# A new order of the front's parts, rests of k and v as two tokens per partition, and squares of eight units summed by VectorE, in a planned attention and mixture kernel

## The chip, the cores and the metric

The kernel runs on one core of a Trainium2 chip. The metric is the time of one execution on the device in microseconds (us), the median of several runs. A profile of one further execution comes with it; its instructions, transfers and waits are what the views below show. Engines are named as in the profile: PE is TensorE (PEld its weight loads), DVE is VectorE, ACT is ScalarE, POOL is GpSimd, SP is SyncE, whose queue issues nearly all transfers (SPq).

## What is computed

Linear attention without a softmax, each row normed, then two feed-forward blocks. The reference, cut to its core (batch 4, 8 heads, 576 tokens, head size 64; 2304 tokens of 512 values, 1024 hidden values, 4 experts; all float32, but the four weights of the first block are float64 on the host):

```python
kv = np.einsum('bhsd,bhse->bhde', k, v)
out = np.einsum('bhsd,bhde->bhse', q, kv)
rms = np.sqrt(np.mean(out * out, axis=-1, keepdims=True) + 1e-06)
x = (out / rms * g_norm)            # then to tokens x (heads, head size)
h = (x @ w1) * (x @ w2) @ w3
x = h @ w_out
p = domain_probs / (domain_probs.sum(-1, keepdims=True) + 1e-09)
for e in range(4):
    y += p[:, e:e + 1] * (np.maximum(x @ e_w1[e], 0.0) @ e_w2[e])
```

## The kernel before

**The planner.** The kernel's work is a list of operations. `Plan.add` (line 110) notes for each the engines that may do it, with a cost in us for each of them, what it reads and writes, and a latency after which its result counts as there. `Plan.order` (line 141) plays these costs through and writes out a fixed order for every engine: an engine that is free takes, of the operations that are ready in that play, the one with the lowest stage, not more than `WINDOW` = 14 stages ahead of the first open one, if the buffers it needs are within their limits (99 tiles of 128x512, 9 of them for attention inputs, 12 for decoded weights, 5 raw weights, 8 PSUM banks). An operation with two possible engines goes to the one that would be done first. On the chip each engine then runs its order from the first to the last, waiting on semaphores where an operand is not there.

**The stages.** `FRONT` (line 37) lists the parts of the first third of the kernel; the place in the list is the stage. A part that needs another one that stands later (a weight, a tile of w_out) makes it then and there, and the later entry does nothing. The parts are:

- `unit b p` (line 691): two heads of batch b. It loads q, k and v of 512 tokens, four per partition (256 KB each), and adds up the outer products k'v on TensorE (`outer`, line 706, the matmuls of line 715). The 64 tokens that 512 leaves over (the rest, `REM`) come from a tile that all units of a batch share. Then q is set by tokens, turned on TensorE, multiplied with k'v (`inner`, line 743) and normed.
- `rest_kv b` (line 565), called by the first unit of a batch: two tiles (k and v), in each of which 64 partitions hold a token and 512 columns hold all eight heads; the other 64 partitions are set to zero by GpSimd. Each load is 512 pieces of 256 bytes.
- `normed_turned` (line 577): squares and their sums per head, `root` on GpSimd (lines 606 and 607), the scaling on VectorE (line 610), turning, and splitting into a high and a low part. While fewer than `SUMMING` = 18 units have been made, and there are 18 with the two of the rests, ScalarE does squares and sums: eight passes over 64 columns, each with an accumulated sum (line 594). In the other branch ScalarE squares 512 columns in one pass and VectorE sums them.
- `rest_unit g` (line 753): the 64 last tokens of two batches.
- `weight n f` (line 909): a 512 KB load of float64 columns of w1 or w2, decoded by ScalarE and VectorE.
- `bilinear_plain`, `bilinear_pair`: the products of x with w1 and w2 (line 325 to 327, three matmuls each for high and low parts), the pair ones by a Strassen-Winograd scheme for two batches; `row`: a row of w3 times w_out; `mixed`, `mixed_product`: the second half of the first block.

Behind the front stand the experts' products, in the order of a loop at the end of the kernel; the planner orders them with the same figures. At the start ten warm-up matmuls are issued (line 422), and PSUM banks that units of stages 1 to 3 take get two or three extra matmuls each (`FILL`, line 1728).

Of the kernel before, what the change touches and what calls it, by code (L numbers as in the profile page):

```python
# [18 lines left out]
P = 128  # L19
# [7 lines left out]
SEVEN = (1,)  # L27
DEFERRED = (0,)
PLAIN = 1
SUMMING = 18  # L30
WARM = 10
FILL = {1: 3, 2: 3, 3: 2}
START = 0.7
# [1 line left out]
BIAS = {"dve": 1.0, "act": 0.0, "pool": 1.0, "pe": 0.0, "sp": 0.0}  # L35

FRONT = (
# [12 lines left out]
)  # L50

class Buf:
# [45 lines left out]
class Plan:  # L98
# [8 lines left out]
        self.limits = dict(limits)  # L107
        self.stage = 0

    def add(self, engines, emit, reads=(), writes=(), latency=0.2, stage=None, free=False, hold=None):  # L110

        op = Op(engines, emit, self.stage if stage is None else stage, latency)
        op.hold = hold
        op.ported = {e for e in engines if e == "pool" or (e == "dve" and not free)}
        op.pinned = stage is not None
        for accesses, write in ((reads, False), (writes, True)):  # L120
            for access in accesses:
                buf, key = access if isinstance(access, tuple) else (access, None)
                if buf not in op.bufs:
                    op.bufs.append(buf)
                    buf.users += 1
                for other, k, w in buf.touched:
                    if other is not op and (write or w) and (k is None or key is None or k == key):
                        op.deps.append(other)
                buf.touched.append((op, key, write))
        op.index = len(self.ops)  # L130
        self.ops.append(op)
        return op
# [128 lines left out]
def attention_moe_kernel(  # L261
# [26 lines left out]
    nc = tc.nc  # L288
    B, H, S, D = q.shape
# [3 lines left out]
    HP = H // 2  # L293
    KD = DM // P
    KF = FF // P
    R = 4
    M = R * P
    REM = S - M
# [12 lines left out]
    add = plan.add  # L311
# [7 lines left out]
    def half(name, dt=F32, ring=None):  # L319
        return Buf("h", name, [P, 512], dt, ring)  # L320
# [8 lines left out]
    def t_act(n, psum=False):  # L329
        return (0.157 if psum else 0.19) + n / 1200  # L330

    def t_dve(n):
        return 0.143 + n / 960
# [10 lines left out]
    def load(buf, *parts, key=None, queue="sp", cost=None):  # L344
        def emit(_):
            for dst, src in parts:
                (nc.sync if queue == "sp" else nc.scalar).dma_start(
                    out=dst(buf.tile), in_=src[:, :] if isinstance(src, Buf) else src
                )

        add(
            {queue: cost or (1.48 if buf.kind == "r" else 0.68)}, emit,
            reads=[src for _, src in parts if isinstance(src, Buf)], writes=[(buf, key)], latency=2.6,
        )

    def spilled(name, buf, value=whole, later=0):
# [192 lines left out]
    kvr = {}  # L549
# [6 lines left out]
    def head_pair(src, b, p):  # L556
        return src[b, 2 * p:2 * p + 2, 0:M, :].rearrange("h (p r) d -> p h r d", r=R)
# [4 lines left out]
    def rest(src, b):  # L562
        return src[b, :, M:S, :].rearrange("h p d -> p h d")

    def rest_kv(b):

        kvr[b] = [half("kvr") for _ in (k, v)]
        for raw, src in zip(kvr[b], (k, v)):
            add({"pool": 0.4}, lambda _, raw=raw: nc.gpsimd.memset(raw[REM:P], 0.0), writes=[(raw, 1)])
            load(  # L570
                raw, (lambda t: t[0:REM].rearrange("p (h d) -> p h d", d=D), rest(src, b)),
                key=0, cost=1.05,
            )

    summed = []

    def normed_turned(ps, places, whole_values=None):
# [4 lines left out]
        t = half("x")  # L582
        ss = Buf("n", "ss", [P, 8, 1], F32)

        summing = SUMMING > len(summed)
        summed.append(t)

        def square(e):
# [25 lines left out]
            )  # L614

        if summing:
            add({"act": 8 * t_act(D, True)}, square, reads=[ps], writes=[t, ss])
        else:
            add({"act": t_act(512, True)}, square, reads=[ps], writes=[t])
            add({"dve": t_dve(512)}, total, reads=[t], writes=[ss], free=True)  # L620
        add({"pool": 1.91}, root, writes=[ss], hold=0.3)
        add({"dve": t_dve(512)}, scale, reads=[ps, ss], writes=[t], free=True)
        pt = turned(t)
        if whole_values is not None:

            def scaled(e):
# [9 lines left out]
                reads=[pt, xscale], writes=[whole_values], free=True,  # L636
# [4 lines left out]
        for n, dst, to, value, key in places:  # L641
# [9 lines left out]
            def low(e, dst=dst, to=to, value=value):  # L651
# [7 lines left out]
                reads=[pt, xscale], writes=[(dst.high, key)], free=True,  # L659
# [5 lines left out]

    def zeroed(name):
        t = half(name)
        add({"pool": 0.5}, lambda _: nc.gpsimd.memset(t.tile, 0.0), writes=[t])
        return t

    def evacuate(dst, src, n, to, value, key=None):
# [19 lines left out]
    def unit(b, p):  # L691
        first = b not in kvb
        if first:
            kvb[b] = zeroed("kvb")
        loaded = []
        for name, src in (("q", q), ("kv", k), ("kv", v)):
            raw = half(name, ring="attention")
            load(raw, (heads, head_pair(src, b, p)), cost=0.82)
            loaded.append(raw)
        qraw, ks, vs = loaded  # L700
        if first:
            rest_kv(b)
        kr, vr = kvr[b]
        ps = bank()

        def outer(e):
            for r in range(R + 1):
                for h in range(2):
                    c = slice(h * D, (h + 1) * D)
                    if r < R:  # L710
                        a, b_ = heads(ks.tile)[:, h, r, :], heads(vs.tile)[:, h, r, :]
                    else:
                        m = slice(p * P + h * D, p * P + (h + 1) * D)
                        a, b_ = kr[:, m], vr[:, m]
                    nc.tensor.matmul(ps[c, c], a, b_, start=r == 0, stop=r == R)  # L715

        add({"pe": 0.9}, outer, reads=[ks, vs, kr, vr], writes=[ps])
        for i in range(2):
            c = slice(i * D, (i + 1) * D)
            evacuate(  # L720
                kvb[b], ps, D, lambda t, i=i, c=c: t[c, p * P + i * D:p * P + (i + 1) * D],
                lambda t, c=c: t[c, c], key=(p, i),
            )
        qs = half("qs")

        def by_token(t):
            return t.rearrange("p (r h d) -> p h r d", r=R, h=2)

        add(
            {"act": t_act(512), "dve": t_fast(512)},  # L730
            lambda e: nc.scalar.copy(by_token(qs.tile), heads(qraw.tile)) if e == "act"
            else nc.vector.tensor_copy(out=by_token(qs.tile), in_=heads(qraw.tile)),
            reads=[qraw], writes=[qs],
        )
        pq = turned(qs)
        qt = half("qt")
        evacuate(qt, pq, 512, whole, whole)
        po = bank()

        def inner(e):  # L740
            for r in range(R):
                c = slice(r * P, (r + 1) * P)
                nc.tensor.matmul(po[:, c], qt[:, c], kvb[b][:, p * P:(p + 1) * P], start=True, stop=True)  # L743

        add({"pe": 0.86}, inner, reads=[qt, (kvb[b], (p, 0)), (kvb[b], (p, 1))], writes=[po])
        xr[b, p] = half("xr")
        if b == B - 1 and p < HP // 2:
            normed_turned(po, [], xr[b, p])
        else:
            xt[b, p] = Pair("xt")  # L750
            normed_turned(po, [(512, xt[b, p], whole, whole, None)], xr[b, p])

    def rest_unit(g):
# [1 line left out]
        load(  # L755
            qraw,
            (lambda t: t[0:REM].rearrange("p (h d) -> p h d", d=D), rest(q, 2 * g)),
            (lambda t: t[REM:P].rearrange("p (h d) -> p h d", d=D), rest(q, 2 * g + 1)), cost=1.5,
        )
        pq = turned(qraw)  # L760
        qs = []
# [999 lines left out]
```

## Time and profile before

| | |
|---|---|
| median of three runs | 1110.79 us (1110.38 to 1113.55) |
| the profiled execution | 1111.78 us |
| its span, first to last instruction | 1110.0 us |
| TensorE busy | 1099.5 us (99%), 6964 matmuls |
| VectorE, ScalarE, GpSimd busy | 824.3, 613.2, 47.1 us |
| mean granted clock of TensorE | 0.997 |
| moved | 282.37 MB in 176866 packets |

The span is what the profile covers; the execution's own time is 1.8 us longer. Busy shares are averages over a kernel with different stages, and a TensorE that counts as busy may be running matmuls that only fill time, or running at a lower clock. So the stages have to be looked at one by one, and the waits beside the busy times.

### The profile page before, as it was taken

The numbers are of one execution on the slowest core, as the hardware profiler recorded it, in microseconds if no ns is written. First come the engines' busy times: TensorE is split into PE (matmuls) and PEld (weight loads), VectorE is DVE, ScalarE is ACT, GpSimd is POOL, SyncE is SP. The second block draws the span as 40 slices with busy tenths as digits, with TensorE's granted clock in tenths as the row PEclk, the third lists the DMA queues.
The fourth block names the chain that finished last, engine by engine and source line by source line (L and its number), as shares of the span: only waits on it lengthen the run. The fifth ranks groups of instructions, "written<-read, shape, count | busy, mean of one in ns | idle before, by whom it ended". The sixth has DMA issues, their size and how long they took to land.

```text
span 1110.0 us, 19707 instructions
## 1 busy us (share of the span) xinstructions
PE 1099.5 (99%) x6964; PEld 1025.2 (92%) x6964; DVE 824.3 (74%) x1698; ACT 613.2 (55%) x1501; POOL 47.1 (4%) x57
## 2 busy tenths in 40 slices
PE   8999999999999999999999999999999999999998
PEld 7888888888888998999999999999999999999998
DVE  5888897889869887888888884456488655464783
ACT  6998744556636655754564465444364545443540
POOL 4513200000000000000000000000000000000000
PEclk9999999999999999999999999999999999999999
DMA  9999993450230499999999997778779787696746
GB/s 288 290 341 331 377 349 110 137 164 25 96 95 29 159 324 354 353 314 299 346 355 361 356 363 242 253 230 275 242 259 350 250 262 263 206 318 200 265 141 201
DMA packets 176866, 282.37 MB, mean 254 GB/s; under 512 B 22144, under 2 KB 89728, under 8 KB 176768
## 3 DMA queue, kind: packets, MB, share of 16 engines
q1 hardware_dynamic: 176448, 280.85, 76.0%
q8 instruction: 55, 0.90, 0.3%
q10 hardware_dynamic: 320, 0.26, 0.1%
q14 instruction: 43, 0.35, 0.1%
HBM read 198.22 MB, written 82.84 MB: 253 GB/s over the span
## 4 chain that ended last, share of the span: by engine, by line
PE 93%; DMA 3%; ACT 2%; DVE 1%; issue 0%; POOL 0%; SPq 0%; ACTq 0%; DVEq 0%
PE b L325 30%; PE b L327 30%; PE b L326 30%; PE b L686 2%; PE b L743 1%; DMA weh<-w 1%; DMA w3raw<-in_moe_w_dram 1%; PE b L715 1%; ACT x L594 0%; DMA w<-w2kept 0%; DMA graw<-in_g_norm_dram 0%; DMA we<-wel 0%; DMA e2raw<-in_moe_w_dram 0%; DMA woraw<-in_moe_w_out_dram 0%; PE b L778 0%
## 5 line engine op out<-in xcount | busy, mean ns | idle before, releaser
L327 PE MATMUL b<-w,htl 128*128 128x256 f32 x756 | 213.6, 283 | 0.0
L325 PE MATMUL b<-w,hth 128*128 128x256 f32 x756 | 213.4, 282 | 0.2 <-DMA w<-w2kept 0.2
L326 PE MATMUL b<-w,hth 128*128 128x256 f32 x756 | 213.5, 282 | 0.0
L674 ACT COPY u<-b 128x384 f32<-128x384 f32 (+1 forms) x191 | 96.2, 504 | 200.8 <-PE b L327 199.4
L1408 DVE TENSOR_TENSOR u<-u,b 128x384 f32<-128x384 f32 x144 | 79.6, 553 | 143.7 <-ACT u L674 74.0
L325 PEld LDWEIGHTS b<-w,hth 128*128 128x128 f32 x756 | 144.1, 191 | 0.6 <-DMA w<-w2kept 0.5
L327 PEld LDWEIGHTS b<-w,htl 128*128 128x128 f32 x756 | 144.5, 191 | 0.0
L326 PEld LDWEIGHTS b<-w,hth 128*128 128x128 f32 x756 | 144.2, 191 | 0.0
L1598 DVE SCALAR_TENSOR_TENSOR acc<-b,pn,acc 128x256 f32<-128x256 f32 x165 | 69.7, 478 | 45.2 <-PE b L327 45.2
L1419 ACT ACTIVATE u<-u 128x384 f32<-128x384 f32 x108 | 56.9, 527 | 65.0 <-DVE u L1408 64.8
L370 ACT CAST hth<-s 128x384 fp32r<-128x384 f32 x144 | 70.6, 511 | 28.4 <-DVE s L1508 26.5
L375 DVE TENSOR_TENSOR htl<-s,hth 128x384 fp32r<-128x384 f32 x144 | 75.4, 550 | 1.6 <-ACT hth L370 1.2
L375 DVE TENSOR_TENSOR htl<-u,hth 128x384 fp32r<-128x384 f32 x108 | 56.1, 551 | 13.5 <-ACT hth L370 13.5
L327 PE MATMUL b<-wdh,htl 128*128 128x512 f32 x144 | 56.7, 394 | 0.0
L326 PE MATMUL b<-wdl,hth 128*128 128x512 f32 x144 | 56.6, 393 | 0.0
L325 PE MATMUL b<-wdh,hth 128*128 128x512 f32 x144 | 56.0, 389 | 0.0
L370 ACT CAST hth<-u 128x384 fp32r<-128x384 f32 x108 | 52.8, 512 | 3.2 <-PE b L327 2.6
L325 PE MATMUL b<-th,weh 128*128 128x512 f32 x112 | 44.6, 398 | 1.1 <-ACT u L674 1.1
L327 PE MATMUL b<-th,wel 128*128 128x512 f32 x112 | 43.7, 390 | 0.0
L326 PE MATMUL b<-tl,weh 128*128 128x512 f32 x112 | 43.7, 390 | 0.0
L954 DVE TENSOR_TENSOR u<-u,b 128x512 f32<-128x512 f32 x42 | 28.6, 686 | 17.1 <-PE b L327 9.2
L1508 DVE TENSOR_TENSOR s<-u 128x384 f32<-128x384 f32 x72 | 38.2, 551 | 0.3 <-ACT u L1419 0.2
(290 smaller groups left out, 3000.2 us busy)
## 6 DMA issues: line engine op xcount, KB each, us to landing
w<-w2kept SPq DMA_DIRECT2D x126, 512.0 KB, 4.4
we<-we SPq DMA_DIRECT2D x240, 256.0 KB, 5.4
we<-weh SPq DMA_DIRECT2D x48, 256.0 KB, 4.1
we<-wel SPq DMA_DIRECT2D x48, 256.0 KB, 4.0
e2raw<-in_moe_w_dram SPq DMA_DIRECT2D x40, 256.0 KB, 4.6
w3raw<-in_moe_w_dram SPq DMA_DIRECT2D x16, 512.0 KB, 3.7
e1raw<-in_moe_w_dram SPq DMA_DIRECT2D x32, 256.0 KB, 4.6
w2kept<-wth SPq DMA_DIRECT2D x32, 256.0 KB, 4.4
```

Source lines behind the costliest of these rows:

```text
L325: nc.tensor.matmul(ps, w[0], x[0], start=first, stop=False, skip_group_check=more)
L326: nc.tensor.matmul(ps, w[0], x[1], start=False, stop=False, skip_group_check=more)
L327: nc.tensor.matmul(ps, w[1], x[0], start=False, stop=last, skip_group_check=more)
L370: nc.scalar.copy(to(dst.high.tile), value(src.tile))
L375: nc.vector.tensor_tensor(out=to(dst.low.tile), in0=value(src.tile), in1=to(dst.high.tile), op=ALU.subtract)
L674: lambda e: nc.scalar.copy(to(dst.tile), value(src.tile)) if e == "act"
L686: nc.tensor.transpose(ps[:, c], raw[:, c], ident)
L954: lambda _: nc.vector.tensor_tensor(out=t.tile, in0=t.tile, in1=ps.tile, op=ALU.add),
L1408: lambda _: nc.vector.tensor_tensor(out=t[:, :W], in0=base[:, :W], in1=ps[:, :W], op=ALU.add),
L1419: lambda eng: nc.scalar.activation(out=t[:, :W], in_=src[:, :W], func=ACTF.Relu)
L1508: lambda eng: nc.vector.tensor_tensor(out=t[:, :W], in0=x[:, :W], in1=y[:, :W], op=op),
L1598: nc.vector.scalar_tensor_tensor(out=a[:, to], in0=ps[:, c], scalar=sc, in1=a[:, to], op0=ALU.mult, op1=ALU.add)
```

## The change

- `FRONT` is a new list. Unit (1, 3) comes before every weight; weight (0, 4) is the first weight; the units of batch 0 stand before those of batches 2 and 3 as before, and unit (2, 2) is the first of these; `bilinear_plain 1 0` stands before `bilinear_plain 0 0`; the rows of w3 begin among the last pair products.
- `rest_kv b j` is called once for two units (j = 0 or 1: four heads) in place of once for four. A partition holds two tokens, 32 partitions hold data, and partitions 32 to 63 and 64 to 127 are cleared in two operations, on GpSimd or VectorE (`cleared`). A load is 128 pieces of 512 bytes, 64 KB. There are 16 such tiles and loads in place of 8, and 32 clearing operations in place of 8.
- The outer product has six rounds per head in place of five, since the rest's two tokens of a partition need a round each.
- `SUMMING` is gone. Units whose number in the order of the list is in `EARLY` (eight of eighteen) take the branch in which VectorE sums; the other ten stay as they were. (The change's own short description has it the other way round: ten units summed by VectorE.)
- The planner's figures: the latency of an operation that TensorE can't do is 0.04 in place of 0.2 us, that of a load 2.1 in place of 2.6; the costs of loads, squares, roots and fills are changed a little.

```diff
-SUMMING = 18
+EARLY = (0, 3, 4, 5, 6, 8, 13, 14)
...
-    "norm_scale, weight 0 7, unit 1 3, unit 1 2, weight 1 4, weight 1 0, unit 1 0, unit 1 1, unit 0 0, "
-    "unit 0 2, unit 0 1, unit 0 3, unit 2 0, bilinear_plain 0 0, weight 0 3, unit 3 1, bilinear_pair 0 3, "
-    "weight 0 4, unit 2 2, weight 1 3, unit 2 3, bilinear_plain 1 0, unit 2 1, bilinear_pair 0 1, unit 3 "
-    "0, rest_unit 0, unit 3 2, bilinear_pair 0 2, weight 1 7, unit 3 3, rest_unit 1, bilinear_pair 1 1, "
-    "bilinear_pair 1 3, weight 0 0, weight 0 5, bilinear_pair 1 0, bilinear_pair 1 2, weight 0 2, row 0, "
...
+    "norm_scale, unit 1 3, weight 0 4, unit 1 2, weight 1 4, unit 1 0, unit 1 1, unit 0 0, weight 1 0, "
+    "unit 0 3, unit 0 1, unit 0 2, unit 2 2, weight 0 3, bilinear_plain 1 0, bilinear_plain 0 0, unit 3 "
+    "0, bilinear_pair 0 3, unit 3 1, unit 2 0, weight 0 1, unit 2 1, unit 2 3, bilinear_pair 0 1, weight "
+    "0 7, rest_unit 0, expert_shares, unit 3 3, unit 3 2, rest_unit 1, bilinear_pair 1 1, bilinear_pair 0 "
+    "2, bilinear_pair 1 2, row 5, weight 0 2, weight 1 3, row 1, bilinear_pair 1 0, w3o_summed 1, row 3, "
+    "row 0, bilinear_pair 1 3, row 2, w_out_tile 0, w_out_tile 2, row 7, row 4, weight 0 5, w_out_tile 7, "
...
-    def add(self, engines, emit, reads=(), writes=(), latency=0.2, stage=None, free=False, hold=None):
+    def add(self, engines, emit, reads=(), writes=(), latency=None, stage=None, free=False, hold=None):
+        if latency is None:
+            latency = 0.2 if "pe" in engines else 0.04
...
-            {queue: cost or (1.48 if buf.kind == "r" else 0.68)}, emit,
-            reads=[src for _, src in parts if isinstance(src, Buf)], writes=[(buf, key)], latency=2.6,
+            {queue: cost or (1.5 if buf.kind == "r" else 0.68)}, emit,
+            reads=[src for _, src in parts if isinstance(src, Buf)], writes=[(buf, key)], latency=2.1,
...
+    def cleared(t, at):
+        add(
+            {"pool": 0.52, "dve": 0.4},
+            lambda e: (nc.gpsimd if e == "pool" else nc.vector).memset(t[at[0]:at[1]], 0.0),
+            writes=[(t, None if at == (0, P) else at)],
+        )
+
+    def rest_kv(b, j):
+        kvr[b, j] = [half("kvr") for _ in (k, v)]
+        for raw, src in zip(kvr[b, j], (k, v)):
+            for at in ((REM // 2, REM), (REM, P)):
+                cleared(raw, at)
             load(
-                raw, (lambda t: t[0:REM].rearrange("p (h d) -> p h d", d=D), rest(src, b)),
-                key=0, cost=1.05,
+                raw,
+                (
+                    lambda t: t[0:REM // 2].rearrange("p (h r d) -> p h r d", h=HP, r=2),
+                    src[b, j * HP:(j + 1) * HP, M:S, :].rearrange("h (p r) d -> p h r d", r=2),
+                ),
+                key=0, cost=0.5,
             )
...
-        summing = SUMMING > len(summed)
+        summing = len(summed) not in EARLY
...
-            add({"act": 8 * t_act(D, True)}, square, reads=[ps], writes=[t, ss])
+            add({"act": 1.75}, square, reads=[ps], writes=[t, ss])
         else:
             add({"act": t_act(512, True)}, square, reads=[ps], writes=[t])
             add({"dve": t_dve(512)}, total, reads=[t], writes=[ss], free=True)
-        add({"pool": 1.91}, root, writes=[ss], hold=0.3)
+        add({"pool": 2.2}, root, writes=[ss], hold=0.3)
...
-            for r in range(R + 1):
+            for r in range(R + 2):
                 for h in range(2):
...
-                        m = slice(p * P + h * D, p * P + (h + 1) * D)
-                        a, b_ = kr[:, m], vr[:, m]
-                    nc.tensor.matmul(ps[c, c], a, b_, start=r == 0, stop=r == R)
+                        at = (p % 2 * 2 + h) * 2 * D + (r - R) * D
+                        a, b_ = kr[:, at:at + D], vr[:, at:at + D]
+                    nc.tensor.matmul(ps[c, c], a, b_, start=r == 0, stop=r == R + 1)
```

## Rows read from the trace of the kernel before

**Rows 1.** The page's busy times, share of the span and instructions of each engine.

```profile
PE 1099.5 (99%) x6964; PEld 1025.2 (92%) x6964; DVE 824.3 (74%) x1698; ACT 613.2 (55%) x1501; POOL 47.1 (4%) x57
```

**Rows 2.** Table by stage: stretch, its length, engines' busy us (instructions), clock, DMA.

```profile
core 0: us, PE busy (x) PEld busy (x) DVE busy (x) ACT busy (x) POOL busy (x), PEclk, DMA share, GB/s
0.00:40.00 40.00, 34.88 (x369) 31.32 (x370) 23.93 (x45) 30.62 (x158) 21.45 (x33) 0.96 1.05 291
10.00:20.00 10.00, 8.81 (x88) 8.09 (x87) 5.56 (x12) 7.22 (x40) 1.91 (x2) 0.83 1.07 344
20.00:30.00 10.00, 8.85 (x113) 7.60 (x110) 7.92 (x14) 9.63 (x51) 6.23 (x6) 1.00 1.13 304
30.00:40.00 10.00, 9.61 (x115) 8.38 (x115) 8.23 (x16) 9.96 (x64) 6.61 (x7) 1.00 1.14 285
40.00:150.00 110.00, 110.00 (x692) 92.72 (x691) 97.60 (x183) 91.55 (x319) 25.68 (x24) 1.00 1.02 340
1080.00:1110.00 30.00, 25.89 (x216) 25.69 (x215) 13.29 (x31) 0.98 (x2) 0.00 (x0) 0.96 0.64 205
```

**Rows 3.** Waits of TensorE from 40 us on: total us, times, longest us.

```profile
PE b L325 <- ACT u L674: 1.1, 2, 0.8
PE b L325 <- DMA w<-w2kept: 0.2, 1, 0.2
```

**Rows 4.** Timeline of TensorE, 6 to 36 us: start, length, instruction, [idle before <-releaser].

```profile
7.41 0.69 PE L715 MATMUL b<-kv 128*64 128x64 f32 x16
9.14 0.34 PE L715 MATMUL b<-kvr 128*64 128x64 f32 x4 [1.05 <-DMA kvr<-in_v_dram]
...
12.80 1.91 PE L743 MATMUL b<-kvb,qt 128*128 128x128 f32 x8
...
20.38 0.69 PE L715 MATMUL b<-kv 128*64 128x64 f32 x16
...
33.14 0.69 PE L715 MATMUL b<-kv 128*64 128x64 f32 x16
...
35.52 0.48 PE L325 MATMUL b<-xth,wh 128*128 128x512 f32 x1
```

**Rows 5.** The chain that ended last, at the first unit's squares: start, length.

```profile
14.75 1.74 ACT x L594 x16
```

**Rows 6.** Timeline of ScalarE, 0 to 16 us.

```profile
10.11 0.62 ACT L370 CAST weh<-val 128x512 fp32r<-128x512 f32 x1 [2.68 <-DVE val L496]
...
14.75 0.22 ACT L594 ACTIVATE x<-b 128x64 f32<-128x64 f32 x1 [2.17 <-PE b L743]
```

**Rows 7.** Transfers from 0 to 40 us: GB/s per us; issues, KB each, us to landing.

```profile
GB/s 0 27 311 330 320 316 221 184 253 343 316 339 351 350 349 351 352 340 349 337 215 171 259 309 348 346 349 350 347 346 341 209 185 204 238 290 343 350 348 345
...
w1raw<-in_moe_w_dram SPq DMA_DIRECT2D x4, 512.0 KB, 8.2
w2raw<-in_moe_w_dram SPq DMA_DIRECT2D x3, 512.0 KB, 7.1
```

**Rows 8.** Groups by shape, whole span (the fills 0 to 36 us): busy us, mean ns.

```profile
L674 ACT COPY u<-b 128x512 f32<-128x512 f32 x47 | 27.6, 588 | 35.6 <-PE b L327 35.2
...
L476 DVE TENSOR_SCALAR val<-val 128x512 f32<-128x512 f32 x40 | 15.9, 420 | 0.0
...
L610 DVE TENSOR_TENSOR x<-b,ss 128x512 f32<-128x512 f32 x18 | 12.4, 688 | 3.3 <-POOL ss L607 3.1
...
L569 POOL MEMSET kvr<- 64x512 f32 x8 | 3.9, 519 | 0.2
```

**Rows 9.** The chain that ended last, at one unit's outer product.

```profile
48.97 0.73 PE b L715 x20
```

**Rows 10.** The chain that ended last, 160 to 203 us.

```profile
161.51 6.74 DMA w3raw<-in_moe_w_dram
...
170.50 0.23 PE b L326
...
198.70 3.73 DMA woraw<-in_moe_w_out_dram
```

**Rows 11.** GpSimd's line 606 alone: duration in ns, least, median, greatest.

```profile
L606 POOL TENSOR_SCALAR ss<-ss x18: 238/454/983, 16.7 to 130.2; 128x8 f32<-128x8 f32 x18
```

More of the change, by code (lines that the diff above doesn't have):

```diff
@@ L563, in rest @@
         return src[b, :, M:S, :].rearrange("h p d -> p h d")
[L565 to L569, printed above, removed]
-            load(
-                raw, (lambda t: t[0:REM].rearrange("p (h d) -> p h d", d=D), rest(src, b)),
-                key=0, cost=1.05,
+    def cleared(t, at):
[9 more added lines that the diff above has]
+                cleared(raw, at)
+            load(
+                raw,
[4 more added lines that the diff above has]
+                key=0, cost=0.5,
             )
@@ L667, in zeroed @@
         t = half(name)
-        add({"pool": 0.5}, lambda _: nc.gpsimd.memset(t.tile, 0.0), writes=[t])
+        cleared(t, (0, P))
         return t
@@ L697, in unit @@
             raw = half(name, ring="attention")
-            load(raw, (heads, head_pair(src, b, p)), cost=0.82)
+            load(raw, (heads, head_pair(src, b, p)), cost=0.75)
             loaded.append(raw)
         qraw, ks, vs = loaded
-        if first:
-            rest_kv(b)
-        kr, vr = kvr[b]
+        if (b, p // 2) not in kvr:
+            rest_kv(b, p // 2)
+        kr, vr = kvr[b, p // 2]
         ps = bank()
         def outer(e):
-            for r in range(R + 1):
+            for r in range(R + 2):
                 for h in range(2):
@@ L757, in rest_unit @@
             (lambda t: t[0:REM].rearrange("p (h d) -> p h d", d=D), rest(q, 2 * g)),
-            (lambda t: t[REM:P].rearrange("p (h d) -> p h d", d=D), rest(q, 2 * g + 1)), cost=1.5,
+            (lambda t: t[REM:P].rearrange("p (h d) -> p h d", d=D), rest(q, 2 * g + 1)), cost=2.0,
         )
```

13 rows, old and new, of the table FRONT are left out of this document.

## The prediction

> **What bounds the kernel now.** I read the page's totals first: TensorE is busy for 1099.5 of 1110.0 us [rows 1], so 10.5 us is all its visible idle time. The table by stage then says where it lies: 5.1 us in the first 40, none from 40 to 150, and 4.1 in the last 30, where the last sums are stored [rows 2]. The list of TensorE's waits has 1.3 us left after 40 us [rows 3]. So nothing before the end can be won except at the start, and there more than the 5.1 us: a busy row of TensorE is no useful row when it fills time. The timeline of the start [rows 4] shows it. The first product of the large matrices starts at 35.52 us. Until then TensorE has only the small matmuls of the attention units, whose outer products (the L715 rows) start at 7.41 us for the first unit, at 20.38 for the fourth, the last of batch 1, and at 33.14 for the eighth. From the fourth to the first large product pass 15 us, in which that unit is normed. The granted clock is also 0.83 between 10 and 20 us [rows 2]; the eight matmuls at 12.80 take 1.91 us, at the lower level of 1.2 GHz for a part of them, right after a stretch in which TensorE waited.
>
> What holds the units back? ScalarE is busy for 9.63 and 9.96 of 10 us between 20 and 40 [rows 2]. Its largest piece per unit is the squares: sixteen records, 1.74 us [rows 5]. Before 14.75 us it idles: 2.68 us for the decoding of the weight that was loaded first, then 2.17 for TensorE [rows 6]. The transfers are the second limit: the queue moves some 300 GB/s without a break from 2 us on, with dips to 184 to 253 just where the rests of k and v pass [rows 7].
>
> **The change, part by part.**
>
> *The order of the front.* Weight (0, 7), 512 KB, leaves the first place on SP's queue, and comes with the pair product that needs it, with its two ScalarE and four VectorE operations of decoding; unit (1, 3) has its place, and weight (0, 4) follows it. Ahead of the last rest of v that the first outer product waits for (1.05 us, until 9.14 [rows 4]) lay 512 + 768 + 256 = 1536 KB; now 768 + 128 = 896 KB. The 640 KB less are 2.1 us at the 311 to 330 GB/s of that stretch [rows 7]. The 2.68 us for which ScalarE stood may come back behind that unit: weight (0, 4) has the same decoding. I take 2.2 us for the earlier start. Bounds: 0, if the ten warm-up matmuls and the constants set the start anyhow, and 4.9, both idle times of ScalarE together [rows 6].
>
> *The squares.* The change's short description has VectorE sum ten units; by the code, the eight numbers in EARLY take the branch with VectorE's sum, and ten of eighteen stay on ScalarE. I go by the code; two more units would take another 2.3 us off ScalarE. Of the first eight units five change (0, 3, 4, 5, 6); of the four of batch 1, which the first large product needs, two. ScalarE's 1.74 us [rows 5] become one pass over 512 columns, 0.59 us by the nearest copy from PSUM [rows 8]: 1.15 less. Two units are 2.3 us, and all five 5.8. VectorE gets a sum over 512 columns each: no row shows this operation; bounds are 0.42 us (its short form over 512 columns, L476) and 0.69 (the long one, L610 [rows 8]). I take 0.69: most of its operations over 512 columns stand there, and the short ones are copies and operations with constants. Five are 3.5 us before 36 us. VectorE has 4.4 + 2.1 + 1.8 us idle from 10 to 40 [rows 2], which covers them; without this cover the 3.5 us come back. The sum waits for ScalarE's pass, GpSimd's root for the sum, and behind the sum on VectorE stand other units' scalings and casts, late by up to its 0.69.
>
> *The two together.* Between 20 and 40 us ScalarE is the queue that everything passes, so an earlier start (2.2) and less work (2.3) add: the first large product 4.5 us earlier, near 31. Bounds: 0, and 7.2 (both idle times, 4.9, and the 2.3).
>
> *Two tokens per partition.* Each outer product has six rounds in place of five. Twenty records take 0.73 us [rows 9], 0.146 a round, which counts in what opens and closes the group. The eight units before the first large product lie in time that TensorE has to spare; the other eight stand in a full TensorE: 8 x 0.146 = 1.2 us lost. Bounds 0 and, for all sixteen, 2.3. The rests now come as 512-byte rows: 256 KB per batch cost 0.95 us of lost flow at 6 to 9 us (221, 184 and 253 against 320 GB/s [rows 7]); half of that is saved, 0.5 us per batch, of which I count nothing apart from the order's 2.2. On SP there are 16 issues in place of 8, each for half the bytes; the transfers behind it never pause in this stretch [rows 7], so an issue more is hidden as long as they queue; taken as 0, bounds 0 and 0.5, the time of one issue.
>
> *Clearing.* Eight fills of 0.52 us [rows 8] become 32, on GpSimd or VectorE as the planner sees fit. GpSimd is busy for 21.45 of the first 40 us [rows 2], so 24 x 0.52 = 12.5 us find room if they don't stand ahead of a root; one that does costs a unit 0.52. Taken as 0, bounds 0 and 1.
>
> *The planner's figures and the list behind 40 us.* A load is thought landed 0.5 us sooner (2.1 for 2.6), results of ScalarE, VectorE and GpSimd 0.16 us sooner. This costs nothing by itself: it reorders. The two waits at 170 and 203 us [rows 3] end in a chain of loads of 6.74 and 3.73 us [rows 10]: the rows of w3 and w_out. The new list puts four rows of w3 ahead of the last pair product, so those loads start under other products. I take half of the 1.1 us: 0.6 gained, bounds 1.1 gained and 1.1 lost.
>
> **The sum.** -4.5 + 1.2 - 0.6 = -3.9 us. The profiled execution took 1111.78 us, its span 1110.0, so 1.8 lie around it; its new time is 1107.9. The median of the runs shown, 1110.79, is 1.0 below it, which gives 1106.9.
>
> **The rivals.**
>
> *Given back* (1110.7). The first large product comes 4.5 us earlier, but TensorE then has little: with weights (0, 4) and (1, 4) only the two products of one column block, 24 matmuls of 0.23 us [rows 10] or 5.5 us, and (1, 0) and (0, 0) come later than before. VectorE, busy for 97.6 of 110 us from 40 to 150 [rows 2], takes over as the queue of the units. Then -0.7 is left of 4.5: 1110.79 - 0.7 + 1.2 - 0.6. For it: VectorE's share; against: from 40 us on TensorE does not wait at all, so there is work in stock.
>
> *GpSimd's fills stop VectorE* (1111.1). Each of 24 fills that meets a short VectorE operation could hold it for up to 0.52 us; if a third do, that is 4.2 us, and the gain is gone (1106.9 + 4.2 = 1111.1). For it: GpSimd's own short operation takes from 238 to 983 ns [rows 11], so the two do meet. Against: in the rows VectorE's operations are not stretched, though all fills there ran while it was idle. The Trainium skill (SBUF — State Buffer, section "SBUF: two separate sides") says of this that GpSimd and a VectorE operation in a two-port mode share one pair of ports by an exclusive lock, and that the loser blocks fully; GpSimd's spread agrees, and no row here shows VectorE as the loser. By that rule the time is this rival's, by the rows alone the forecast's.
>
> *Late loads* (1114.4, slower). The plan now trusts a load 0.5 us earlier, while in the front weights land 7.1 to 8.2 us after their issue [rows 7]. TensorE's stream is in order: a product placed ahead of its operand stops all behind it, in the pair products and the rows of w3. Each costs about the 0.5 us of the figure (the longest seen was 0.8 [rows 3]). It decides from some 8 such stops (4 us, gain gone); 15 make 7.5 us and 1106.9 + 7.5 = 1114.4. For it: the two stops of before ended in loads. Against: only two in 1070 us, at a queue with much the same figures.
>
> **How the numbers follow.** The forecast 0.54, given back 0.22, fills 0.05, late loads 0.19. 0.3% (3.3 us) is about what a measurement of this kernel can tell from no change. Of the forecast's 0.54 about 0.05 falls within it (over 1107.5), so faster 0.49; same 0.05 + 0.22 + 0.05 - 0.01 = 0.31; slower 0.20. All bounds on the good side together (7.2 and 1.1 us gained, 0 lost) give 1102.5; the range begins 0.5 below, for runs that differ, and ends at 1114, just short of the middle of the late loads, so about 0.15 lies outside. The likeliest case alone has 1103.5 to 1109.
>
> **What would show it.** The first unit's outer product no longer waits at 9 us and ends before 8; the first large product starts at 30 to 32 us; ScalarE's square records fall from 144 to 80, and eight VectorE sums of some 0.69 us appear; L715 has 384 records, and TensorE stays full from 40 to 150 us. Wrong would be: the first large product at 35 again (then ScalarE was not what held it); an early start with idle or thin TensorE time between 32 and 60 (given back); VectorE operations of 0.42 us stretched to 0.9 (fills); waits of TensorE for loads beyond 40 us that sum to over 4 us (late loads).

## The result and the profile after

The changed kernel takes 1127.76 us in the median (1126.66 to 1128.13, four runs) by 1111.25 for the kernel before: a ratio of 1.0144, 95% interval 1.0126 to 1.0161. It is 16 us slower where 3.9 us less had been forecast, and outside the range. In the comparisons below the kernel before had medians of 1111.0 to 1112.7 us, so parts are compared by ratios, and us are ratios times 1111. The intervals make the difference between two such ratios good to some 3 us where each kernel has four runs, and to some 2 us with ten.

The page's totals and the table by stage of the changed kernel (columns as in [rows 1] and [rows 2]):

```profile
span 1125.7 us, 19771 instructions
PE 1104.3 (98%) x7028; PEld 1028.9 (91%) x7028; DVE 838.8 (75%) x1719; ACT 608.2 (54%) x1389; POOL 47.5 (4%) x60
```

```profile
0.00:40.00 40.00, 29.08 (x322) 26.55 (x322) 26.31 (x51) 22.86 (x75) 16.80 (x28) 0.91 1.00 282
20.00:30.00 10.00, 6.09 (x67) 5.57 (x68) 7.46 (x15) 4.13 (x14) 6.96 (x9) 0.66 1.10 291
100.00:200.00 100.00, 97.05 (x526) 81.35 (x524) 84.39 (x159) 59.20 (x153) 10.69 (x10) 0.98 0.87 294
380.00:650.00 270.00, 266.63 (x1478) 246.12 (x1477) 223.89 (x490) 152.47 (x314) 0.00 (x0) 1.00 0.96 327
```

The same two later stretches of the kernel before, which the prediction had not set out:

```profile
100.00:200.00 100.00, 99.25 (x541) 84.68 (x539) 84.67 (x159) 60.80 (x167) 10.39 (x10) 1.00 0.79 276
380.00:650.00 270.00, 269.77 (x1493) 250.45 (x1492) 223.64 (x486) 152.62 (x315) 0.00 (x0) 1.00 0.99 338
```

TensorE's idle time grew in three places: from 5.1 to 10.9 us in the first 40 us, from 0.75 to 2.95 between 100 and 200, and from 0.2 to 3.4 between 380 and 650. That is 11.1 of the 15.7 us by which the span grew; the sixth round of the outer products (24 records in 0.85 us, the first line below, in place of 20 in 0.73 [rows 9]) adds 0.12 us to each of sixteen products, 1.9 in all where each counts, and some of the rest is time at a lower granted clock behind the waits (0.66 between 20 and 30 us).

```profile
37.72 0.85 PE b L729 x24
```

The start, in the timeline of TensorE and then of VectorE; they answer to [rows 4] and to the VectorE that the prediction counted as idle:

```profile
9.79 0.45 PE L729 MATMUL b<-kvr 128*64 128x64 f32 x8 [1.81 <-DVE kvr L570]
...
23.54 1.12 PE L700 MATMUL b<-ident,x 128*128 128x128 f32 x4 [6.00 <-DVE x L624]
...
42.61 0.48 PE L327 MATMUL b<-xth,wh 128*128 128x512 f32 x1
```

```profile
1.54 0.48 DVE L570 MEMSET kvr<- 32x512 f32 x1 [0.16 <-issue]
7.68 0.15 DVE L429 TENSOR_SCALAR g<-graw 128x1 f32<-128x1 f32 x1 [5.65 <-DMA graw<-in_g_norm_dram]
8.00 1.74 DVE L570 MEMSET kvr<- 64x512 f32 x3 [0.16 <-issue]
9.90 2.38 DVE L570 MEMSET kvr<- 32x512 f32 x4 [0.16 <-issue]
12.42 0.48 DVE L570 MEMSET kvb<- 128x512 f32 x1 [0.15 <-issue]
13.07 6.05 DVE L570 MEMSET kvr<- 32x512 f32 x10 [0.16 <-issue]
...
19.50 0.68 DVE L614 TENSOR_REDUCE ss<-x 128x8 f32<-128x512 f32 x1
```

VectorE has 21 of the 38 clearing operations: the change lets it do the six of whole tiles (`kvb`, `qr`) too. Two run at once; then its queue comes to the scaling of g_norm and waits 5.65 us for that transfer, with everything behind it. From 8.00 to 19.12 us it clears: 18 operations, some 0.62 us from one to the next. The first unit's squares begin on ScalarE at 12.04 us, 2.7 us earlier than before [rows 5], and were done at 12.64, but the sum starts at 19.50. TensorE, with nothing but units to work on, waits 1.81 us for a cleared tile and 6.00 for that unit, and the first large product starts at 42.61 us where it was 35.52.

The later loss is another thing. TensorE's waits from 100 us on (total us, times, longest), and ScalarE's timeline around the longest of them:

```profile
PE b L327 <- ACT u L688: 5.5, 6, 2.3
PE b L327 <- DMA w<-w2kept: 0.8, 1, 0.8
```

```profile
179.64 0.59 ACT L688 COPY u<-b 128x512 f32<-128x512 f32 x1 [1.00 <-PE b L329]
185.79 0.69 ACT L464 ACTIVATE val<-woraw 128x512 f32<-128x512 f32 x1 [5.56 <-DMA woraw<-in_moe_w_out_dram]
...
188.09 0.57 ACT L688 COPY u<-b 128x512 f32<-128x512 f32 x1
```

A load of w_out, issued from 179.99 us on, is not there before 185.7; ScalarE has its decoding next in its order and waits 5.56 us, and behind it stands the copy of line 688 that frees TensorE's bank. So TensorE waits "for ScalarE", which itself waits for a load.

### The profile page after: what moved, and what is told of

It reads as the page before. It is cut to its first block, busy times and chain, and to the rows that moved or that the text cites. A ratio compares the mean times of both kernels' runs of the same rounds, so it can differ in the third digit from the quotient of the medians.

```text
span 1125.7 us, 19771 instructions
## 1 busy us (share of the span) xinstructions
PE 1104.3 (98%) x7028; PEld 1028.9 (91%) x7028; DVE 838.8 (75%) x1719; ACT 608.2 (54%) x1389; POOL 47.5 (4%) x60
## 4 chain that ended last, share of the span: by engine, by line
PE 90%; DMA 4%; DVE 2%; ACT 1%; issue 1%; SPq 0%; POOL 0%; ACTq 0%; DVEq 0%; POOLq 0%
PE b L327 29%; PE b L329 29%; PE b L328 29%; PE b L700 2%; PE b L757 1%; DMA e2raw<-in_moe_w_dram 1%; PE b L729 1%; DVE kvr L570 1%; DMA woraw<-in_moe_w_out_dram 1%; DMA w2raw<-in_moe_w_dram 1%; DMA w<-w2kept 1%; DMA graw<-in_g_norm_dram 0%; DMA w<-wel 0%; DMA e1raw<-in_moe_w_dram 0%; ACT u L688 0%
## 5 line engine op out<-in xcount | busy, mean ns | idle before, releaser
L377 DVE TENSOR_TENSOR wel<-s,weh 128x512 fp32r<-128x512 f32 x48 | 32.4, 685 | 8.3 <-ACT weh L372 6.8
```

What stands on the lines that cost most here:

```text
L377: nc.vector.tensor_tensor(out=to(dst.low.tile), in0=value(src.tile), in1=to(dst.high.tile), op=ALU.subtract)
```

## The experiments

Theory 1: VectorE's clearing operations make the start late. Theory 2: it is loads that land later than planned, the start hardly matters. The first three runs keep the changed kernel's plan, and change only what an operation issues.

**e1, clearing on GpSimd.**

```diff
-            lambda e: (nc.gpsimd if e == "pool" else nc.vector).memset(t[at[0]:at[1]], 0.0),
+            lambda e: nc.gpsimd.memset(t[at[0]:at[1]], 0.0),
```

> The changed kernel with the same plan, but every clearing operation is issued on GpSimd, also the 21 that the plan gives to VectorE. Theory 1 (VectorE's clearing operations, in its queue ahead of the first unit's sum, make the start late): VectorE's sum of the first unit starts near 13 to 14 us in place of 19.5, the first large product before 37 us in place of 42.6, and the kernel takes about 1121 to 1122 us, 6 less than the changed one. Theory 2 (loads that land later than planned make the loss, the start hardly matters): 1126 to 1128 us.

1120.93 us, ratio 1.0081 (1.0058 to 1.0104). VectorE's sum starts at 12.37, and the first large product at 37.22, two rows of this run's timelines:

```profile
12.37 0.69 DVE L614 TENSOR_REDUCE ss<-x 128x8 f32<-128x512 f32 x1 [0.73 <-ACT x L604]
```

```profile
37.22 0.48 PE L327 MATMUL b<-xth,wh 128*128 128x512 f32 x1
```

So some 7.0 us of the 16 go with VectorE's clearing operations, theory 1: TensorE is idle for 7.4 of the first 40 us in place of 10.9, and its clock there is 1.00 in place of 0.91. GpSimd clears until 14.54 us in this run, and its first root starts at 14.63; so it holds the root by some 1.6 us behind the sum, which still costs less than the sum at 19.50 did.

**e2, the scaling late.** The scaling of g_norm is issued ahead of the first operation that reads it.

```diff
-        nc.vector.tensor_scalar(out=g8, in0=graw, scalar1=float(D) ** 0.5, scalar2=None, op0=ALU.mult)
+        g8_late.append(lambda: nc.vector.tensor_scalar(
+            out=g8, in0=graw, scalar1=float(D) ** 0.5, scalar2=None, op0=ALU.mult
+        ))
...
+            if g8_late and op.emit is not load_norm and xscale in op.bufs:
+                g8_late.pop()()
             op.emit(e)
```

> The changed kernel with the same plan, but VectorE's scaling of g_norm is issued just ahead of its first reader, so that VectorE does not wait 5.65 us for that transfer with its clearing operations behind. Theory 1a (the wait and the clearing operations together make the start late): VectorE is through with its clearing operations near 14 us, the first unit's sum starts near 14 in place of 19.5 us, the first outer product does not wait 1.8 us, and the kernel takes about 1122 to 1123 us. Theory 1b (the clearing operations alone do): the sum starts at 17 us or later, and no more than 2 us are won. Theory 2: 1126 to 1128 us.

1123.02 us, ratio 1.0093 (1.0060 to 1.0125). In VectorE's timeline the clearing runs without a break and the sum starts at 13.66 (line numbers are four higher here):

```profile
1.54 2.37 DVE L574 MEMSET kvr<- 32x512 f32 x4 [0.16 <-issue]
...
7.23 6.06 DVE L574 MEMSET kvr<- 32x512 f32 x10
...
13.66 0.68 DVE L618 TENSOR_REDUCE ss<-x 128x8 f32<-128x512 f32 x1
```

Without the wait the same clearing operations do little harm: they pass while VectorE has nothing else. It took both, theory 1a.

**e3, both edits.**

> Both edits of the two runs before. Theory 1: no more than with the clearing operations on GpSimd alone, about 1121 us; the first large product before 37 us. What is left above the kernel before, about 10 us, then lies behind 40 us: some 2 us for the sixth round of the outer products, some 7 for waits from 120 us on. Theory 2: 1126 to 1128 us.

1121.18 us, ratio 1.0088 (1.0066 to 1.0110): the two repair the same thing. TensorE is idle for 5.25 us of the first 40, as in the kernel before. The first unit's product with k'v starts at 9.60 us in place of 12.80 [rows 4], but the first large product at 35.72, no earlier than before:

```profile
9.60 1.06 PE L761 MATMUL b<-kvb,qt 128*128 128x128 f32 x8
...
35.72 0.48 PE L327 MATMUL b<-xth,wh 128*128 128x512 f32 x1
```

The rest of the loss, 9.8 us, lies behind.

**e4, the latencies of before**, in the changed kernel as it is; this plans anew.

```diff
-    def add(..., latency=None, stage=None, free=False, hold=None):
-        if latency is None:
-            latency = 0.2 if "pe" in engines else 0.04
+    def add(..., latency=0.2, stage=None, free=False, hold=None):
...
-            ... writes=[(buf, key)], latency=2.1,
+            ... writes=[(buf, key)], latency=2.6,
```

> The changed kernel planned with the latencies of before (0.2 us for every result, 2.6 us for a load); this plans anew, so the order differs everywhere. Theory 3 (the shorter latencies place products ahead of late loads): TensorE's stalls from 120 us on fall from some 7 us to 2 or less, and the kernel takes about 1122 us, still with the late start. Rival (the list places them so, whatever the latencies): 1126 to 1128 us.

1123.59 us, ratio 1.0105 (1.0081 to 1.0128), 4.3 us less, with the start still late (a wait of 6.5 us for a unit's scaling). TensorE's waits behind 100 us fall from 6.3 to 3.1 us, not to the 2 that had been expected. So the planner's latencies have a share of their own; that the start hardly matters, the other half of theory 2, is ruled out by e1 and e2.

**e5, all three edits together.**

> The changed kernel with the clearing operations issued on GpSimd, VectorE's scaling of g_norm issued late, and planned with the latencies of before. If the late start (some 6 us) and the late loads (some 6 us) are two causes that add, it takes 1115 to 1117 us: 1111, 2 to 3 for the sixth round of the outer products, and 2 for the rows of w3 near 190 us. If they are one (each repair only shifts the same work), it takes 1120 us or more.

1117.16 us, ratio 1.0038 (1.0023 to 1.0053). The causes add, within the noise: 6.2 us for the clearing alone (e3) and 4.3 for the latencies alone (e4) make 10.5, and together the edits bring 11.8. In this order the latencies' part is 5.6. The table by stage, e3 first and then e5, shows which stage each repairs:

```profile
0.00:40.00 40.00, 34.75 (x400) 31.26 (x401) 23.61 (x41) 29.13 (x89) 32.91 (x53) 1.00 1.01 280
100.00:200.00 100.00, 94.49 (x470) 78.68 (x467) 83.12 (x159) 58.20 (x150) 10.71 (x10) 0.98 0.85 287
380.00:650.00 270.00, 267.68 (x1486) 247.74 (x1485) 226.04 (x497) 150.78 (x309) 0.00 (x0) 1.00 0.98 332
```

```profile
0.00:40.00 40.00, 34.38 (x395) 31.57 (x396) 20.61 (x38) 28.19 (x95) 31.01 (x51) 0.96 0.98 280
100.00:200.00 100.00, 97.81 (x551) 82.71 (x550) 88.49 (x169) 62.16 (x158) 10.25 (x8) 1.00 0.86 301
380.00:650.00 270.00, 269.75 (x1493) 250.32 (x1492) 224.45 (x494) 150.86 (x310) 0.00 (x0) 1.00 0.98 337
```

With the latencies of before TensorE's idle time falls from 5.5 to 2.2 us between 100 and 200 and from 2.3 to 0.25 between 380 and 650. The first large product starts at 40.12 us in e5, 4.4 us later than in e3, and yet the time is shorter: its start alone does not set the time.

**e6 to e9, one part alone on the kernel before.** e6: the new list. e7: `summing = len(summed) not in (0, 3, 4, 5, 6, 8, 13, 14)`. e8: the changed `rest_kv` and outer product, with all clearing on GpSimd in the plan too. e9: the changed latencies (the inverse of e4's edit).

> The kernel before with the new list alone. If the list itself is bad for the chip (the rows of w3 and w_out among the last pair products, weight (1, 0) and (0, 0) later), it takes 1115 us or more, with a stall of 2 us or more between 170 and 200 us. If it is good and only the other parts spoil it, 1106 to 1109 us, with the first large product 2 us earlier than the 35.5 us of before.

1118.5 us, ratio 1.0050 (1.0033 to 1.0066). The list is worse by itself. In the profile, of a run of 1121.2 us, TensorE is idle for 7.2 of the first 40 us in place of 5.1 and for 3.1 between 100 and 200 us in place of 0.75; its waits from 100 us on:

```profile
PE b L325 <- ACT u L674: 4.0, 3, 1.9
```

It puts rows of w3, and with the first of them the loads of w_out, among the last pair products, which reload weights at the same time, and ScalarE waits 7.7 us for loads of w_out between 165 and 200 us. What the list costs at the start isn't explained by that.

> The kernel before with VectorE summing the squares of the eight units, alone. By the forecast's term for ScalarE (1.15 us less for a unit, two units ahead of the first large product) the first large product comes 2 us earlier and the time is 1108 to 1110 us. If ScalarE was not what held the units, or VectorE's queue takes back what ScalarE's gives, 1110.5 to 1113.

1113.27 us, ratio 1.0011 (0.9998 to 1.0024): no gain, and the first large product at 38.68 us in place of 35.52, while the sum of the first unit was done by 15.4.

> The kernel before with the rests as two tokens per partition alone, all clearing on GpSimd also in the plan. The sixth round costs 0.12 us in each of sixteen outer products, so 1112 to 1113 us with a start as early as before; if the smaller loads let the first units start sooner, up to 1 us less; if 32 clearing operations on GpSimd hold its roots, 1115 or more, with the first large product after 37 us.

1115.47 us, ratio 1.0032 (1.0017 to 1.0046), 3.5 us, more than the 1.9 of the sixth round. The profile is of a run of 1122.3 us, 6.8 above the median. The first large product starts at 42.47 us in it, after 37 as one branch of the expectation had it, but the reason given there is not borne out: TensorE waits for copies on ScalarE and VectorE (3.1 and 2.0 us), only 0.3 for a cleared tile, and GpSimd is idle for 1.91 us before its first root. What makes the other 1.6 us isn't settled.

> The kernel before planned with the changed latencies alone (0.04 us for results of ScalarE, VectorE and GpSimd, 2.1 us for a load). If the shorter latencies by themselves place work ahead of late loads, TensorE's stalls behind 380 us grow from some 2 us to 4 or more and the time is 1114 to 1117 us. If they do harm only with the new list, 1110 to 1113.

1118.55 us, ratio 1.0046 (1.0029 to 1.0063), but its runs spread from 1113.7 to 1120.3. The profile is of the run of 1113.7, and still has 1.7 us of idle TensorE between 380 and 650 in place of 0.2; the 4 us or more behind 380 us that had been expected are not in it. The latencies do harm without the new list.

**e10 to e12.** e10: e2's edit on the kernel before. e11: a load's latency 4.5 in place of 2.6 on the kernel before. e12: e5 with the list of before.

> The kernel before, same plan, with VectorE's scaling of g_norm issued ahead of its first reader. VectorE then does not stand until 7.6 us, but before that time it has nothing but the decoding of weight (0, 7), which ends some 2 us earlier. If an earlier start is worth its time at the end, 1109 to 1110 us; if the start's gain is given back later (VectorE 97.6 of 110 us busy from 40 to 150 us), as with the early sums, 1111 to 1113, no difference.

1111.56 us, ratio 0.9995 (0.9983 to 1.0007): no difference in time. But VectorE's wait was not idle waiting: the decoding of the first weight stood behind it, and with it ScalarE's 2.68 us [rows 6]. In e10 the first unit's squares start at 13.04 us in place of 14.75:

```profile
13.04 0.22 ACT L598 ACTIVATE x<-b 128x64 f32<-128x64 f32 x1 [0.98 <-PE b L747]
```

The first large product starts at 35.09 in place of 35.52. So 1.7 us at the first unit are 0.4 at the first large product, and none at the end that can be seen.

> The kernel before planned with 4.5 us for a load in place of 2.6, nearer to what the trace shows from issue to landing (3.7 to 6.6 us). If late loads cost the plan time, the two stops at 170 and 203 us and those at 440 to 500 us shrink, and the time is 1107 to 1109 us, better than both kernels. If the list was fitted to 2.6, the new order loses elsewhere: 1112 us or more.

1111.06 us, ratio 0.9990 (0.9979 to 1.0001). Between the two expectations: TensorE has only 0.2 us of waits left behind 100 us in its list, where it had 1.3, and the gain is 1 us, too small to be told from none.

> The changed kernel with clearing on GpSimd, late scaling, the latencies of before and the list of before: what is left of the change are the rests by two, the eight sums and the small costs. If the list is what is left of the loss (5.6 us alone on the kernel before), it takes 1111 to 1113 us. If the rests are (3 us alone), 1114 to 1116.

1114.31 us, ratio 1.0018 (1.0007 to 1.0030): the time lies in the second expectation, by the ratio (1113.0 us) it is between the two, so both parts count: of the 4.2 us that e5 left, 2.2 go with the list, 2.0 stay with the rests by two, the early sums and the small costs. Neither is known to better than half of it.

**e13 to e15.** e13: e3 with 4.5 us for a load, results at 0.04. e14: the changed kernel with `"dve": 0.63` in place of 0.4 in `cleared`. e15: e10 and e11 together.

> The changed kernel with clearing on GpSimd and late scaling, and a planned latency of 4.5 us for a load in place of 2.1; results of ScalarE, VectorE and GpSimd stay at 0.04. If the load's figure makes the waits behind 100 us, they fall from 7.6 us (with both repairs alone) to 2 or less, and the time is 1114 to 1117 us, as with both latencies of before. If the results' figure does, the waits stay at 5 us or more and the time is 1119 to 1122.

1117.34 us, ratio 1.0053 (1.0032 to 1.0073). In the profile, of a run of 1115.6 us, the waits of line 327 behind 100 us fall to 0.9 us, where e3 has 7.6; 2.3 us for a unit stand there in this order, so 3.2 in all, between the two expectations:

```profile
PE b L704 <- DVE x L628: 2.3, 1, 2.3
PE b L327 <- ACT u L692: 0.5, 1, 0.5
PE b L327 <- DMA w<-w2kept: 0.4, 1, 0.4
```

So a long enough figure for loads brings 3.9 of the 5.6 us, with that of results left as changed; the ratio is at the upper end of e5's interval. As 4.5 is more than the 2.6 of before, and no run changes the figure of results alone, how the 5.6 us divide between the two figures isn't shown.

> The changed kernel with one figure of the plan changed: a clearing operation on VectorE costs 0.63 us, as the trace shows from one to the next, in place of 0.4. The plan then gives VectorE 4 of them in place of 21. If that figure is what made the start late, the first unit's sum starts near 12 to 14 us, and the time is 1120 to 1123 us. If the start stays late by the other parts, 1126 to 1128.

1122.09 us, ratio 1.0102 (1.0077 to 1.0127). One figure of the plan brings 4.7 us back (one of the four runs took 1127.0, the others 1121.4 to 1122.7): VectorE gets 4 clearing operations in place of 21, and the first sum starts at 12.35.

```profile
12.35 0.69 DVE L614 TENSOR_REDUCE ss<-x 128x8 f32<-128x512 f32 x1
```

> The kernel before with late scaling of g_norm and 4.5 us for a load, the two small gains that the runs so far point to (each about 1 us, within the noise). If they add: 1109 to 1110 us by the 1111 of before. If they are noise or are given back: 1111 to 1113.

1110.75 us, ratio 0.9988 (0.9976 to 1.0000). By the ratio it is the fastest of the kernels tried, 1.3 us under the kernel before and 0.2 under e11; its interval ends at 1, so that it beats the kernel before is not shown. It beats the changed kernel clearly.

## Why the prediction was wrong

- **Clearing: "taken as 0, bounds 0 and 1". This is the step that failed first**, with 7.0 us (e1) in place of 0. The step weighed only GpSimd's room and its roots. The diff allows VectorE at 0.4 us; the trace had no clearing on VectorE, and the step took no bound for it. Measured, one takes 0.485 us and starts 0.62 after the one before; at the planned 0.4 the planner sent 21 of 38 there, and with 0.63 it sends 4 (e14). The prediction also missed what was queued ahead of them on VectorE: the scaling of g_norm, which waits for a transfer until past 7.5 us. That wait stood in the trace of before, where taking it away changed nothing in the time (e10); the change put 18 operations behind it, and the first unit's sum behind those.
- **The planner's figures: "this costs nothing by itself".** They cost 5.6 us (e3 to e5), and 5.1 alone (e9). The rival of the late loads had the mechanism and too small a chance (0.19). Its place was not quite right: in the longest stop the load holds ScalarE's decoding, and the copy behind that, and only so TensorE; 0.8 of the 6.3 us are TensorE's own wait for a load.
- **The rows of w3 and w_out: 0.6 us gained.** The two stops at 170 and 203 us [rows 3] did go, but a longer one, of 2.3 us, ended at 188.72. The list alone loses 5.6 us (e6), and 2.2 where all else is repaired (e5 to e12).
- **The squares: 2.3 us off the first large product.** ScalarE's work did fall (80 square records on line 608 in place of 144), and VectorE's eight sums cost 682 ns each, the 0.69 that was taken. But alone the part gains nothing (e7): the first large product came later, and the time did not fall. A busy share of 96 to 100% on ScalarE had been read as the bound; less of its work did not bring the units through sooner in the order that the planner then made.
- **The earlier start: 2.2 us.** It came for the first unit and got lost behind it: with both repairs the first unit's outer product no longer waits and its product with k'v starts 3.2 us earlier, but the first large product does not (e3: 35.72 us). So the step that failed is that the two add up at the first large product; adding 2.2 and 2.3 there took ScalarE for the queue that everything passes. In e3 ScalarE is idle for 0.9 of the 10 us before 40, TensorE for none of them: it is full with the units' own small matmuls. The 2.68 us of [rows 6], too, were read as the time of a decoding; e10 shows that it was VectorE's wait for g_norm. What would have to change for the units to come through sooner stays open.
- **Two tokens per partition: 1.2 us.** The round costs 0.12 us where 0.146 had been worked out; in sixteen units 1.9. Alone the part costs 3.5 (e8), of which 1.6 are open.
- **GpSimd's fills stop VectorE** was a rival with the wrong engine: VectorE's own fills did. That GpSimd's fills stretch VectorE's operations is seen, in a few places and in the repaired kernels: in e14 an operation of 0.42 us on VectorE took 0.71 at 11.71 us while GpSimd, at 11.45, took 0.69 for a clearing of 0.52, and in e3, where GpSimd clears from 1.87 to 14.50 us, one took 0.84, near the 0.9 that was named as the sign:

```profile
10.24 0.84 DVE L482 TENSOR_SCALAR val<-val 128x512 f32<-128x512 f32 x1 [10.24 <-ACT val L468]
```

That agrees with the rule of the shared ports (the Trainium skill, SBUF — State Buffer, "SBUF: two separate sides"), by which a GpSimd operation and a VectorE operation in a two-port mode hold them one at a time; the mode of these operations no trace shows. The 80 operations of these two kinds (lines 482 and 489) take 33.8 us in e3 by 32.0 in the kernel before (lines 476 and 483), so on them it costs less than 2 us of VectorE's time in the whole kernel, and not the 4.2 of the rival.

Undone one after another, the parts are 6.2 us (clearing, e3), 5.6 (latencies, e5), 2.2 (list, e12) and 2.0 left. They make the 16.0 because each is the difference to the run before it; in another order the shares would differ, as the parts alone do, since each new plan orders everything anew. The first two are good to some 3 us, the third to some 2. The forecast lacked these 16.0, but for the 1.2 of the round, and had 5.1 us of gains (4.5 and 0.6) that did not come.

## What to carry to other kernels

An operation that may run on a second engine is a change to that engine's queue: before its cost is put at nothing, look at what that queue waits for first, and at what it has to do next. A planner takes every cost that is too low as an invitation; put in the distance from one start to the next that the trace shows, not the length of one operation (e14). For a load, try the time to landing under the traffic of its stage: it helped in e13, and in the kernel before (e11) the gain could not be told from none. An operation that comes earlier is worth nothing until it is followed to the end: here 3.2 us at the first unit were gone at the first large product. A wait that costs nothing today may cost as soon as something is put behind it.

## What the runs showed of the hardware

- A clearing operation costs the same for 32, 64 or 128 partitions of 512 float32: 485 ns on VectorE, some 520 on GpSimd. On VectorE the next one starts some 0.62 us after; between them it is idle for up to 0.16 us, which the trace puts down to the issue:

```profile
L570 DVE MEMSET kvr<- 64x512 f32 x10 | 4.8, 485 | 1.4 <-issue 0.3
L570 DVE MEMSET kvr<- 32x512 f32 x9 | 4.4, 485 | 1.3 <-issue 0.5
L570 DVE MEMSET kvb<- 128x512 f32 x2 | 1.0, 485 | 1.1 <-PEq L1759 0.9 <-issue 0.2
```

- TensorE's wait that ended at 188.72 us cost more than its own 2.3 us. After it the matmuls of 512 columns went at 0.43 us and then at 0.23 again (the chain that ended last); from 189.4 to 192.8 us the granted clock was 0.50, the lower of the two levels, 1.2 GHz. The nine matmuls from 189.44 on that took 0.28 to 0.43 us in place of 0.23 cost some 1.6 us more:

```profile
189.40:192.80 3.40, 3.40 (x10) 2.63 (x9) 1.73 (x3) 0.92 (x2) 0.00 (x0) 0.50 0.82 250
```

```profile
189.83 0.43 PE b L327
...
192.39 0.43 PE b L327
192.81 0.28 PE b L328
193.09 0.23 PE b L329
```
